# Key indicators by one unsigned comparison, mask rows by DMA, weights in quarters, and where x is transposed, in a fused block-sparse attention and feed-forward kernel

## The chip, the core and the metric

The kernel runs on one NeuronCore of a Trainium2 chip. A core has five engines that run side by side, each with its own instruction queue: TensorE (PE, matrix products, and transposes as products with an identity), VectorE (DVE), ScalarE (ACT, activation functions), GpSimd (POOL) and SyncE (SP, which here only issues transfers). Sixteen DMA engines move data; a transfer is issued from the queue of SP, POOL or ACT and then runs by itself. Matrix products write to PSUM, a small memory of banks that PE, DVE and ACT share; the rest lies in SBUF, 128 partitions wide.

The metric is device time in microseconds (us), the median of several runs.

## What is computed

Attention over four batches of eight heads, 768 positions of 64 numbers each, followed by a gated feed-forward layer. A key block of 32 positions is visible from a query block if it is a neighbour, if either is the first or the last of the 24 blocks, or if it is one of three sampled blocks.

```python
def _attn_ref(q, k, v, sampled_blocks):          # q, k, v: 4 x 8 x 768 x 64
    scores = scale * np.matmul(q, k.transpose(0, 1, 3, 2))
    mask = np.abs(blk_i - blk_j) <= 1
    mask = mask | (blk_i == 0) | (blk_j == 0) | (blk_i == 23) | (blk_j == 23)
    for qb in range(24):
        for kb in sampled_blocks[qb]:
            mask[qb * 32:(qb + 1) * 32, kb * 32:(kb + 1) * 32] = True
    attn = softmax(np.where(mask, scores, -1e9))
    return np.matmul(attn, v)

def _moe_ref(x, w_gate, w_val, w_out, rms_g):    # x: 3072 x 512; w_gate, w_val: 512 x 1536
    xn = x / np.sqrt(np.mean(x * x, axis=-1, keepdims=True) + 1e-06) * rms_g
    g = xn @ w_gate
    return (g * sigmoid(g) * (xn @ w_val)) @ w_out
```

## The kernel before

**Groups.** The queries are worked through in nine groups (L51): three of 256 queries for batch 0 (groups 0, 1, 2), then two of 384 for each other batch. Each group runs its eight heads in order (the loop at L545 to L626). For a head, `scores` (L289) multiplies keys by queries into a PSUM tile `st` and ACT takes the exponential into `ex`. One head later, `pv` (L305) multiplies `ex` by the values `Vp` (whose last column is ones, so that the softmax sum comes out as well), and DVE divides into `stage`.

**The mask is part of the product.** `KT` and `QT` hold 64 rows of keys or queries and 24 further rows. In `KT` these are indicators (row r is 1 where the key lies in block r), in `QT` they are 0 where block r may be seen and -65536 where not. So one product over 88 rows gives masked scores. The positions are interleaved: column s of chunk c stands for position 6 s + c. The rows are built once, in head 0 of the first buffer: `kind` by `mask_keys` (L206, L208) from an integer table `ki_i` that POOL's iota makes (L160), `qmask` by `mask_queries` (L213, L216) from `qnat`, which comes from the small 24 x 24 table `bm` (L184 to L197). Then they are copied to the other seven heads, by DVE (`copy_rows`, L220, L222) or by DMA on SP's queue (L246, L475), and to the second buffer, which batches 1 and 3 use, by two DMAs (L480).

**The head of the kernel.** Batch 0's first two heads of keys and queries come by their own loads and are cast by ACT and turned by PE (`first_cast`, `first_turn`, `first_copy`; `first` in L114 to L119); the other heads of batch 0 come by POOL's queue, which casts on the way (`load_qk`, L72), and are turned by PE in `transpose_qk` (L250, copies at L266) during group 0. Values come by `load_v` (L80) and are cast by DVE in `cast_v` (L103). The weights `wg`, `wv` come in two halves each (`load_gv`, L93), `wo` in one. All loads of one queue keep their order. `keep_busy` (L146) issues products that nobody reads (`unread`), where PE would be idle; `thin` (L557) says in which heads.

**The feed-forward layer as filling.** A group's x is ready when its last head has been divided. `squares` (L319) sums its squares on DVE, `rms_power` (L327) takes the power on POOL, and `rms_scale` (L335 ff.) scales it on DVE into `xs`. Then `xs` has to be turned, so that features lie on partitions, into `xg`. Groups 0, 1 and the last do this on PE (`transpose_x`, L352: eight or twelve transposes in two halves, with the scale `rmsg` applied in DVE's copies at L365); the others scale by `gain` too (L342) and let a DMA on SP's queue transpose (L345). `enter` (L438) then puts the group's feed-forward pieces (`gate`, `val`, `down`; L376, L386, L402) into the list `fill`, and `position()` (L443), called four times a head, takes pieces from it at the rate that empties the list in the given number of positions. So PE alternates between the next group's attention and the last group's feed-forward layer. What is left of the last group runs at the end.

**The order is written by hand** (`manual_schedule`, L58): each engine executes its instructions in program order and waits only for what it needs. An instruction that waits holds up all behind it on its engine.

**Places that the change touches.** In group 0: the prologue (L155 to L247), head 0's turn of the second head (L563 to L574), `side_work` (L461), and the copies in head 2 (L598). In group 1: x of group 0, whose two scalings come at the end of head 0 (L620 to L623) and whose transposes come at the end of head 1 (`tx` is 1 there, L554, L601, L609), with 36 positions. In group 3: x of group 2, by DMA (`by_dma`, L335).

Of the kernel before, what the change touches and what calls it, by code (L numbers as in the profile page):

```python
# [11 lines left out]
I32 = mybir.dt.int32  # L12
AF = mybir.ActivationFunctionType
ALU = mybir.AluOpType
# [3 lines left out]
def kernel(  # L18
# [71 lines left out]
    NWC = 2  # L90
    WC = DFF // NWC

    def load_gv(j):  # L93
        for t, src in ((wg, moe_w_gate), (wv, moe_w_val)):
            nc.gpsimd.dma_start(
                out=t[:, :, j * WC:(j + 1) * WC],
                in_=src.rearrange("(c p) f -> p c f", p=P)[:, :, j * WC:(j + 1) * WC])
# [58 lines left out]
    nc.gpsimd.iota(kq_i[0:NB, :], pattern=[[1, NB]], base=0, channel_multiplier=-1)  # L156
    kc_i = const.tile([32, 1], I32, name="kc_i")
    nc.gpsimd.iota(kc_i[0:NB, :], pattern=[[0, 1]], base=0, channel_multiplier=1)
    ki_i = const.tile([32, S], I32, name="ki_i")
    nc.gpsimd.iota(ki_i[0:NB, :], pattern=[[1, NB], [0, 32]], base=0, channel_multiplier=-1)  # L160
# [6 lines left out]
    load_gv(0)  # L167
# [3 lines left out]
    for i in range(2):  # L171
# [4 lines left out]
    mid = (NB - 1) / 2.0  # L176
    nc.vector.tensor_scalar(out=rg[0:NB, :], in0=kc[0:NB, :], scalar1=-mid, scalar2=None,
                            op0=ALU.add)
    nc.vector.tensor_tensor(out=rg[0:NB, :], in0=rg[0:NB, :], in1=rg[0:NB, :], op=ALU.mult)
    nc.vector.tensor_scalar(out=rg[0:NB, :], in0=rg[0:NB, :], scalar1=(mid - 0.25) ** 2,  # L180
                            scalar2=None, op0=ALU.is_ge)
    kq = const.tile([32, NB], FP32, name="kq")
    nc.vector.tensor_copy(out=kq[0:NB, :], in_=kq_i[0:NB, :])
    bm = const.tile([32, NB], FP32, name="bm")  # L184
    nc.vector.tensor_tensor(out=bm[0:NB, :], in0=kq[0:NB, :], in1=kq[0:NB, :], op=ALU.mult)
    nc.vector.tensor_scalar(out=bm[0:NB, :], in0=bm[0:NB, :], scalar1=1.5, scalar2=rg[0:NB, :],
                            op0=ALU.is_le, op1=ALU.max)
    nc.vector.memset(bm[0:NB, 0:1], 1.0)
    nc.vector.memset(bm[0:NB, NB - 1:NB], 1.0)
    samp = const.tile([32, NB, NRND], FP32, name="samp")  # L190
# [12 lines left out]
    kind = KT[0][D:KR, 0, :]  # L203
    qmask = QT[0][D:KR, 0, :]

    def mask_keys(lo, hi):  # L206

        nc.vector.tensor_scalar(  # L208
            out=kind.rearrange("p (c r) -> p c r", c=NC)[:, lo:hi, :],
            in0=ki_i[0:NB, :].rearrange("p (r c) -> p c r", c=NC)[:, lo:hi, :],  # L210
            scalar1=0.0, scalar2=None, op0=ALU.is_equal)

# [14 lines left out]
    mask_keys(0, HC)  # L227
    unread2 = ps_s.tile([P, 2, 512], FP32, name="unread0", tag="st")
    unread = unread2[:, 0, :]
    for _ in range(4):  # L230
        keep_busy(1, 256, unread)
        for e in range(2):
            nc.tensor.matmul(out=unread2[:, e, 0:256], lhsT=idle[e * D:(e + 1) * D, 0:P],
                             rhs=idle[e * D:(e + 1) * D, 0:256], start=True, stop=True)
# [11 lines left out]
    nc.sync.dma_start(out=KT[0][D:KR, 6:H, :],  # L246
                      in_=kind.unsqueeze(1).to_broadcast([NB, H - 6, S]))  # L247
# [87 lines left out]
    def by_dma(e):  # L335
        return e["grp"] not in (groups[0], groups[1], groups[-1])
# [124 lines left out]
    def side_work(gi, h):  # L461

        if gi == 0:
            if h == 0:
                copy_rows(KT, kind, 2, 4, 0, S)
                copy_rows(QT, qmask, 2, 4, 0, 2 * P)
            if h % 2 == 0:
                cast_v(0, h // 2, nc.vector)
            if h == 1:
                load_gv(1)  # L470
                nc.gpsimd.dma_start(out=wo, in_=moe_w_out.rearrange("(c p) f -> p c f", p=P))
# [6 lines left out]
            if h == 5:  # L478
                for T, m in ((KT, kind), (QT, qmask)):
                    nc.sync.dma_start(out=T[1][D:KR, :, :],  # L480
# [197 lines left out]
```

## Time and profile before

| what | us |
|---|---|
| median of three runs (lowest, highest) | 315.83 (315.8, 316.31) |
| the profiled execution, its own time | 317.69 |
| span of that execution in the profile | 315.9 |
| PE busy (share of the span) | 305.8 (97%) |
| DVE busy | 205.5 (65%) |
| ACT busy | 207.4 (66%) |
| POOL busy | 47.3 (15%) |
| first scores of group 0 on PE | 6.27 |
| transposes of x of group 0 on PE | 28.78 |
| first gate product | 30.26 |
| gate product of group 2 | 83.60 |

The page of a profile gives busy time by engine, the chain of work that ended last (followed back from the last instruction, at each step to what released it), and groups of instructions by line, engine and tile: busy time, mean duration of one in ns, and how long the engine sat idle before them and for whom. The timeline lists instructions in order: start in us, duration in us, engine, line, operation, output and inputs with their shapes, how many are merged, and in brackets the idle time before and what ended it. PEld is the loading of a product's stationary operand, which overlaps other products. SPq is a transfer issued by SP. In the list of stretches each line is: the stretch, its length, and for PE, PEld, DVE, ACT and POOL the busy time (with instructions in brackets), then PE's granted clock, the share of the DMA engines that were busy (above 1 means that packets overlap) and GB/s. Lines beginning with q1 give a hardware DMA queue in a window: packets, MB, busy share of 16 engines. The unread products count as busy too.

### The profile page before, as it was taken

Reading aid. Unit: us, or ns where it says so; the run is one execution under the profiler, and the core shown is the slowest. Engines: PE = TensorE matmul, PEld = TensorE weight load, DVE = VectorE, ACT = ScalarE, POOL = GpSimd, SP = SyncE. Lnnn points to the kernel's source line nnn. Section 1 sums busy time; section 2 is a strip of 40 time slices with the busy share of each in tenths; the row PEclk is TensorE's granted clock in tenths of the full one; section 3 lists DMA queues with packets and bytes.
Section 4 is the critical chain, followed back from the end, with each engine's and each line's share of the span. In section 5 each row is a group of like instructions: output and inputs, shape, how many; then the busy total and the mean of one; then the engine's idle time right before and its main releaser. Section 6 shows DMA issues by size and latency. Waiting matters only on the chain.

```text
span 315.9 us, 7285 instructions
## 1 busy us (share of the span) xinstructions
PE 305.8 (97%) x2869; PEld 200.5 (63%) x2869; DVE 205.5 (65%) x563; ACT 207.4 (66%) x336; POOL 47.3 (15%) x70
## 2 busy tenths in 40 slices
PE   8888999999899999999999999999999999989995
PEld 4566886886588556655666566655666566645653
DVE  7987875678367657682767457683767546683860
ACT  6687776677688676676766766766767666722331
POOL 9705221000220122012020122010000100010000
PEclk9999999999999999999999999999999999999999
DMA  7999999997779487705784288814000230002002
GB/s 143 297 242 212 209 247 188 162 201 131 190 134 164 86 183 152 133 20 130 160 163 100 50 192 125 152 38 118 33 2 0 48 105 2 3 0 100 2 0 101
DMA packets 66766, 37.24 MB, mean 118 GB/s; under 512 B 49532, under 2 KB 62444, under 8 KB 66732
## 3 DMA queue, kind: packets, MB, share of 16 engines
q1 hardware_dynamic: 53000, 19.59, 29.2%
q0 software_dynamic: 13696, 17.17, 28.6%
q8 instruction: 22, 0.36, 0.5%
q14 instruction: 12, 0.10, 0.1%
q10 hardware_dynamic: 36, 0.01, 0.0%
HBM read 28.59 MB, written 6.29 MB: 110 GB/s over the span
## 4 chain that ended last, share of the span: by engine, by line
PE 89%; DVE 7%; DMA 2%; ACT 1%; issue 1%; POOL 0%; DVEq 0%; ACTq 0%
PE gp L379 20%; PE vp L390 19%; PE st L298 19%; PE yp L407 18%; PE op L310 11%; DVE junk L322 2%; DMA xg<-xs 2%; PE unread L151 1%; PE tx L361 1%; DVE stage L315 1%; ACT ex L301 1%; DVE KT L208 0%; DVE u L394 0%; PE tqk L261 0%; DVE KT L266 0%
## 5 line engine op out<-in xcount | busy, mean ns | idle before, releaser
L301 ACT ACTIVATE ex<-st 128x768 bf16<-128x768 f32 x192 | 154.4, 812 | 58.1 <-PE st L298 56.0
L298 PE MATMUL st<-QT,KT 88*128 88x384 bf16 (+1 forms) x432 | 94.6, 309 | 0.8 <-ACT ex L301 0.4
L394 DVE SCALAR_TENSOR_TENSOR u<-th,gp 128x384 bf16<-128x384 bf16 (+1 forms) x108 | 54.8, 508 | 43.1 <-ACT th L383 41.5
L379 PE MATMUL gp<-xg,wg 128*128 128x384 bf16 (+1 forms) x432 | 80.4, 307 | 1.2 <-DMA xg<-xs 1.2
L390 PE MATMUL vp<-xg,wv 128*128 128x384 bf16 (+1 forms) x432 | 80.1, 307 | 0.4 <-DVE u L394 0.4
L407 PE MATMUL yp<-wo,hps 128*128 128x512 bf16 (+1 forms) x300 | 74.0, 370 | 0.7 <-DVE hps L396 0.7
L383 ACT ACTIVATE th<-gp 128x384 bf16<-128x384 f32 (+1 forms) x108 | 48.9, 453 | 28.0 <-PE gp L379 27.8
L396 DVE TENSOR_TENSOR hps<-u,vp 128x384 bf16<-128x384 bf16 (+1 forms) x108 | 55.1, 510 | 11.7 <-PE st L298 0.5
L298 PEld LDWEIGHTS <-KT 88*128 88x128 bf16 x432 | 41.6, 98 | 26.9 <-DVE QT L222 1.3
L379 PEld LDWEIGHTS <-wg 128*128 128x128 bf16 x432 | 40.2, 97 | 21.9 <-DMA xg<-xs 1.3
L390 PEld LDWEIGHTS <-wv 128*128 128x128 bf16 x432 | 40.5, 97 | 20.8 <-issue 0.8
L310 PEld LDWEIGHTS <-ex 128*128 128x128 bf16 x1152 | 46.1, 98 | 11.5 <-DVE stage L315 1.3
L310 PE MATMUL op<-Vp,ex 128*128 128x65 bf16 x1152 | 48.8, 194 | 1.1 <-DVE stage L315 0.6
L407 PEld LDWEIGHTS <-hps 128*128 128x128 bf16 x300 | 27.7, 97 | 23.7 <-DVE hps L396 1.2
L314 DVE RECIPROCAL rz<-op 128x3 f32<-128x3 f32 (+1 forms) x72 | 12.5, 173 | 29.0 <-PE op L310 28.8
L330 POOL TENSOR_TENSOR rstd<-ssq,mhalf 128x3 f32<-128x3 f32 (+1 forms) x9 | 7.3, 814 | 150.0 <-DVE ssq L322 150.0
L315 DVE TENSOR_TENSOR stage<-op,rz 128x192 bf16<-128x192 f32 (+1 forms) x72 | 24.1, 335 | 2.5
L413 ACT ACTIVATE yo<-yp 128x512 f32<-128x512 f32 (+1 forms) x25 | 14.4, 577 | 17.0 <-PE yp L407 17.0
L83 POOL DMA_DIRECT2D vraw<-in_v_dram x16 | 12.0, 748 | 70.9 <-DVE Vp L104 70.7
L322 DVE CUSTOM_DVE_ANT_0 junk<-stage 128x448 bf16<-128x448 bf16 x24 | 14.9, 623 | 0.6
L342 DVE SCALAR_TENSOR_TENSOR xs<-stage,rstd,gain 128x512 bf16<-128x512 bf16 x17 | 11.8, 748 | 4.5 <-POOL rstd L330 4.4
L151 PE MATMUL unread<-idle 128*128 128x512 bf16 (+1 forms) x37 | 12.6, 391 | 1.2 <-DVE idle L144 1.2
(61 smaller groups left out, 98.7 us busy)
## 6 DMA issues: line engine op xcount, KB each, us to landing
vraw<-in_v_dram POOLq DMA_DIRECT2D x16, 384.0 KB, 4.9
out_dram<-yo SPq DMA_DIRECT2D x23, 256.0 KB, 2.3
kbf<-in_k_dram POOLq DMA_DIRECT2D x15, 192.0 KB, 6.2
qbf<-in_q_dram POOLq DMA_DIRECT2D x15, 192.0 KB, 6.5
KT<-turned SPq DMA_DIRECT2D x24, 96.0 KB, 3.6
QT<-turned SPq DMA_DIRECT2D x24, 96.0 KB, 2.4
wg<-in_moe_w_gate_dram POOLq DMA_DIRECT2D x2, 768.0 KB, 16.4
wv<-in_moe_w_val_dram POOLq DMA_DIRECT2D x2, 768.0 KB, 20.2
```

Of the source, the lines that this page charges most:

```text
L151: nc.tensor.matmul(out=t[:, 0:cols], lhsT=idle[:, 0:P], rhs=idle[:, 0:cols], start=True, stop=True)
L298: nc.tensor.matmul(out=at[:, e, 0:tg], lhsT=KT[b % 2][0:KR, h, jt * P:(jt + 1) * P], rhs=QT[b % 2][0:KR, h, c0 * P:c0 * P + tg], start=Tru ...
L301: nc.scalar.activation(out=ex[:, nj * part:nj * (part + 1), :], in_=at[:, 0:nj, 0:tg], func=AF.Exp, scale=SCALE)
L310: nc.tensor.matmul(out=op[:, it, 0:VW], lhsT=ex[:, jt, it * P:(it + 1) * P], rhs=Vp[b % 2][:, h, jt, :], start=(jt == 0), stop=(jt == NC - 1))
L315: nc.vector.tensor_tensor(out=stage[:, 0:n, h * D:(h + 1) * D], in0=op[:, 0:n, 0:D], in1=rz[:, 0:n].unsqueeze(2).to_broadcast([P, n, D]), ...
L322: nc.vector.tensor_tensor_reduce(out=junk[:, 0:hi - lo], in0=part, in1=part, scale=1.0, scalar=(e["ssq"][:, it:it + 1] if lo else DM * 1e- ...
L379: nc.tensor.matmul(out=gp[:, 0:tg], lhsT=wg[:, c, f * P:(f + 1) * P], rhs=xg[:, c, 0:tg], start=(c == 0), stop=(c == KD - 1))
L383: nc.scalar.activation(out=th[:, 0:tg], in_=gp[:, 0:tg], func=AF.Tanh, scale=0.5)
L390: nc.tensor.matmul(out=vp[:, 0:tg], lhsT=wv[:, c, f * P:(f + 1) * P], rhs=xg[:, c, 0:tg], start=(c == 0), stop=(c == KD - 1))
L394: nc.vector.scalar_tensor_tensor(out=u[:, 0:tg], in0=th[:, 0:tg], scalar=1.0, in1=gp[:, 0:tg], op0=ALU.add, op1=ALU.mult)
L396: nc.vector.tensor_tensor(out=hps[:, f, 0:tg], in0=u[:, 0:tg], in1=vp[:, 0:tg], op=ALU.mult)
L407: nc.tensor.matmul(out=yp, lhsT=hps[:, f, tt * P:(tt + 1) * P], rhs=wo[:, f, lo:hi], start=(f == 0), stop=(f == NF - 1))
```

## The change

- **Tables.** Three integer tables of POOL's are made with other bases, and one is added (`kw_i`), so that read as unsigned numbers one comparison says whether a value lies in a range: |a - b| <= 1 becomes (a - b + 1) <= 2 unsigned. In `ki_i` the order of elements becomes that of `kind`, so it is read without a stride.
- **Order in the prologue.** The first half of the indicators is computed ahead of the sampled blocks' part; eight full unread products replace twelve, of which eight used half the rows.
- **Mask rows.** Query rows of the first 256 columns go to heads 2 to 7 by one DMA on SP's queue, issued after `mask_queries(0)`; DVE's copies of them (heads 2 and 3 in head 0, 4 to 7 in head 2) go. The key rows' DMA takes heads 4 to 7 instead of 6 and 7; DVE's copy for 4 and 5 goes. The rows of the second buffer are moved from SP's queue in group 0, head 5, to POOL's queue in group 2, head 1.
- **Turn of the second head.** DVE's row copies for head 1 come ahead of the turn's copies, and one of the four copies is ACT's.
- **`rmsg`** is scaled at the end of group 0 instead of in head 0.
- **Weights.** The first halves of `wg` and `wv` come in two quarters each.
- **x of group 0** is scaled in heads 0 and 1 of group 1 and turned at the start of head 2 (both halves at once), again with 36 positions; head 2 is `thin` too. **x of group 2** is turned by PE.

```diff
-    def load_gv(j):
+    def load_gv(lo, hi):
...
-                out=t[:, :, j * WC:(j + 1) * WC],
+                out=t[:, :, lo * P:hi * P],
...
-    nc.gpsimd.iota(kq_i[0:NB, :], pattern=[[1, NB]], base=0, channel_multiplier=-1)
+    nc.gpsimd.iota(kq_i[0:NB, :], pattern=[[1, NB]], base=1, channel_multiplier=-1)
...
+    nc.gpsimd.iota(kw_i[0:NB, :], pattern=[[0, 1]], base=-1, channel_multiplier=1)
...
-    nc.gpsimd.iota(ki_i[0:NB, :], pattern=[[1, NB], [0, 32]], base=0, channel_multiplier=-1)
+    nc.gpsimd.iota(ki_i[0:NB, :], pattern=[[1, NC], [NC, P]], base=0,
+                   channel_multiplier=-32)
...
-    load_gv(0)
+    load_gv(0, NF // 4)
+    load_gv(NF // 4, NF // 2)
...
-    nc.vector.tensor_scalar(out=rg[0:NB, :], in0=kc[0:NB, :], scalar1=-mid, scalar2=None,
-                            op0=ALU.add)
-    nc.vector.tensor_tensor(out=rg[0:NB, :], in0=rg[0:NB, :], in1=rg[0:NB, :], op=ALU.mult)
-    nc.vector.tensor_scalar(out=rg[0:NB, :], in0=rg[0:NB, :], scalar1=(mid - 0.25) ** 2,
+    nc.vector.tensor_scalar(out=rg[0:NB, :], in0=kw_i[0:NB, :].bitcast(U32), scalar1=NB - 2.5,
                             scalar2=None, op0=ALU.is_ge)
-    nc.vector.tensor_copy(out=kq[0:NB, :], in_=kq_i[0:NB, :])
-    nc.vector.tensor_tensor(out=bm[0:NB, :], in0=kq[0:NB, :], in1=kq[0:NB, :], op=ALU.mult)
-    nc.vector.tensor_scalar(out=bm[0:NB, :], in0=bm[0:NB, :], scalar1=1.5, scalar2=rg[0:NB, :],
-                            op0=ALU.is_le, op1=ALU.max)
+    nc.vector.tensor_scalar(out=bm[0:NB, :], in0=kq_i[0:NB, :].bitcast(U32), scalar1=2.5,
+                            scalar2=None, op0=ALU.is_le)
+    nc.vector.tensor_scalar(out=bm[0:NB, :], in0=bm[0:NB, :], scalar1=rg[0:NB, :],
+                            scalar2=None, op0=ALU.max)
...
+            in0=ki_i[0:NB, :].bitcast(U32).rearrange("p (c r) -> p c r", c=NC)[:, lo:hi, :],
+            scalar1=31.5, scalar2=None, op0=ALU.is_le)
+
+    mask_keys(0, HC)
...
-    mask_keys(0, HC)
-    unread2 = ps_s.tile([P, 2, 512], FP32, name="unread0", tag="st")
...
+    nc.sync.dma_start(out=QT[0][D:KR, 2:H, 0:2 * P],
+                      in_=qmask[:, 0:2 * P].unsqueeze(1).to_broadcast([NB, H - 2, 2 * P]))
+    unread = ps_s.tile([P, 1024], FP32, name="unread0", tag="st")
+    keep_busy(8, 256, unread)
...
-    nc.sync.dma_start(out=KT[0][D:KR, 6:H, :],
-                      in_=kind.unsqueeze(1).to_broadcast([NB, H - 6, S]))
+    nc.sync.dma_start(out=KT[0][D:KR, 4:H, :],
+                      in_=kind.unsqueeze(1).to_broadcast([NB, H - 4, S]))
...
-        return e["grp"] not in (groups[0], groups[1], groups[-1])
+        return e["grp"] not in groups[:FIRST] and e["grp"] != groups[-1]
...
-                copy_rows(QT, qmask, 2, 4, 0, 2 * P)
...
-                load_gv(1)
+                load_gv(NF // 2, NF)
...
-            if h == 5:
-                for T, m in ((KT, kind), (QT, qmask)):
-                    nc.sync.dma_start(out=T[1][D:KR, :, :],
-                                      in_=m.unsqueeze(1).to_broadcast([NB, H, S]))
...
+        if gi == 2 and h == 1:
+            for T, m in ((KT, kind), (QT, qmask)):
+                nc.gpsimd.dma_start(out=T[1][D:KR, :, :],
+                                    in_=m.unsqueeze(1).to_broadcast([NB, H, S]))
...
-        tx = 1 if gi == 1 else TX
...
+                copy_rows(KT, kind, 1, 2, 0, S)
+                copy_rows(QT, qmask, 1, 2, 0, 2 * P)
                 for which in range(2):
                     for w in range(2):
                         first_copy(1, which, second[which], w, 0, 1 if which else HC,
-                                   nc.vector.tensor_copy)
-                copy_rows(KT, kind, 1, 2, 0, S)
-                copy_rows(QT, qmask, 1, 2, 0, 2 * P)
-                nc.vector.tensor_scalar(out=rmsg, in0=rmsg, scalar1=float(DM) ** 0.5,
-                                        scalar2=None, op0=ALU.mult)
+                                   nc.scalar.copy if w > which else nc.vector.tensor_copy)
...
-            if h == tx and ending is not None and tx > 1:
+            if h == TX and ending is not None:
                 transpose_x(ending, 0)
+                if gi == 1:
+                    transpose_x(ending, 1)
+                    enter(ending, NPOS + 4)
+                    ending = None
...
-            if gi == 0 and h == 2:
-                copy_rows(KT, kind, 4, 6, 0, S)
-                copy_rows(QT, qmask, 4, H, 0, 2 * P)
-            if h == tx == 1 and ending is not None:
-                transpose_x(ending, 0)
...
+            if gi == 0 and h == H - 1:
+                nc.vector.tensor_scalar(out=rmsg, in0=rmsg, scalar1=float(DM) ** 0.5,
+                                        scalar2=None, op0=ALU.mult)
```

## The prediction

> **What bounds the kernel.** I read the share of busy time first, then the chain that ended last, then busy time by stretch, then the timeline where that shows TensorE (PE) idle.
>
> ```profile
> PE 89%; DVE 7%; DMA 2%; ACT 1%; issue 1%; POOL 0%; DVEq 0%; ACTq 0%
> ...
> L379 PE MATMUL gp<-xg,wg 128*128 128x384 bf16 (+1 forms) x432 | 80.4, 307 | 1.2 <-DMA xg<-xs 1.2
> ...
> L361 PE MATMUL tx<-ident,xs 128*128 128x128 bf16 x8 | 0.8, 222 | 1.2 <-DVE xs L348 1.2
> ```
>
> PE carries the end. Its waits are small, and two of them are for x: 1.2 us for the DMA that transposes it, 1.2 us for the DVE scaling ahead of PE's own transposes. By stretch:
>
> ```profile
> 28.00:30.00 2.00, 1.03 (x12) 0.86 (x13) 1.86 (x7) 0.25 (x1) 2.00 (x4) 1.00 1.17 216
> 30.00:32.00 2.00, 2.00 (x27) 1.67 (x26) 1.17 (x5) 1.79 (x3) 1.96 (x3) 1.00 1.16 207
> ```
>
> The first number after the length is PE's busy time. From 30.4 us PE is full but for 0.4 us near 46.4, 0.9 us at 82.7 and 0.3 us at 112. Before it, PE also runs dummies, so "busy" proves nothing; there the chain goes through DVE. So two questions: how much earlier does the first gate product end, and what changes later. In the head of the kernel:
>
> ```profile
> 4.86 0.82 DVE L208 TENSOR_SCALAR KT<-ki_i 24x384 bf16<-24x384 int32 x1
> ...
> 6.24 0.82 DVE L208 TENSOR_SCALAR KT<-ki_i 24x384 bf16<-24x384 int32 x1
> ...
> 7.10 1.02 SPq L246 DMA_DIRECT2D KT<-KT  x1
> ...
> 8.11 0.72 DVE L141 COPY KT<-tfirst 64x384 bf16<-64x384 bf16 x2 [1.04 <-PE tfirst L132]
> ...
> 10.07 0.50 PE L298 MATMUL st<-QT,KT 88*128 88x256 bf16 x3 [0.32 <-DVE QT L222]
> ...
> 13.00 0.11 PEld L298 LDWEIGHTS <-KT 88*128 88x128 bf16 x2 [0.47 <-DVE KT L266]
> ...
> 15.02 1.10 DVE L104 CAST Vp<-vraw 128x768 bf16<-128x768 f32 x1
> ...
> 17.62 0.22 PEld L298 LDWEIGHTS <-KT 88*128 88x128 bf16 x3 [0.48 <-DVE QT L222]
> ```
>
> The scores of heads 1, 2 and 4 (10.07, 13.0, 17.6 us) all wait for DVE's copies of mask rows or keys. And at the two places of x:
>
> ```profile
> 28.37 0.77 DVE L348 TENSOR_SCALAR xs<-stage,rstd 128x512 bf16<-128x512 bf16 x2
> 28.78 0.23 PE L361 MATMUL tx<-ident,xs 128*128 128x128 bf16 x1 [0.99 <-DVE xs L348]
> ...
> 29.59 1.12 DVE L365 TENSOR_SCALAR xg<-tx,rmsg 128x256 bf16<-128x256 bf16 x4
> ```
> ```profile
> 79.76 2.58 SPq L345 DMA_TRANSPOSE xg<-xs  x2
> ...
> 83.60 0.61 PE L379 MATMUL gp<-xg,wg 128*128 128x256 bf16 x4 [0.91 <-DMA xg<-xs]
> ```
>
> **The change, part by part.**
>
> *Indicators.* On DVE four small operations go (pieces of the chain: 0.17, 0.19, 0.12, 0.20 = 0.68 us), one maximum of 24x24 comes (nearest row, the fused one at 2.46: 0.23; take 0.20). Saved 0.48. The key comparison reads contiguously instead of every sixth integer: between 0.28 (half of the 768-element qnat row of 0.55) and 0.82 (no gain); I take 0.45, a little over half the strided cost. The first one moves ahead of the sampled blocks and fills what was saved, so the query mask still ends at 4.94 us; then the turn's copies start at 4.97 instead of 5.71, and the second comparison ends at 6.05 instead of 7.06. The first scores hardly profit: seven dummies of 0.21 us from 4.68 hold PE until 6.16 (scores were at 6.27), and ScalarE's second cast ends at 6.39. Gain 0.1. The fewer dummies ahead are a wash: eight at 0.327 us between starts stand for four rounds of 0.65.
>
> *Head 0 to head 1.* The row copies for head 1 (0.35 + 0.35) now fill DVE's 1.04 us idle before the turn. After the turn (about 8.0) DVE has 0.36 + 0.22 + 0.24, to 8.85; ScalarE has one key copy (row 0.47, or 0.36), behind both exponentials, to about 9.1. The dummies ahead of head 1 (0.43) may take the bank which that copy reads: scores at 9.2 to 9.6 instead of 10.07.
>
> *Head 2, by V.* DVE copies rows for heads 2 and 3 (0.55, to 9.4) and then waits for V of the first pair: issued 3.92, landed 6.1 later, 10.0; one more iota ahead of it on POOL's queue (0.1) and more mask packets beside it make 10.3. Cast 0.57, key copies 1.14: 12.0 instead of 12.96.
>
> *Head 2, by masks.* Query rows for heads 2 to 7 now come through SP's queue, issued about 4.95: 24 rows x 6 heads = 144 packets of 512 B, with no row like it. Near bound: the first loads landed 2.5 to 3.7 us after issue, so 8.7. Far bound: the KT transfer above, issued 7.10, 48 packets, moved only here (windows of 1 us from 11 and from 12):
>
> ```profile
> q1 hardware_dynamic: 21, 0.03, 8.5%
> ...
> q1 hardware_dynamic: 39, 0.04, 14.3%
> ```
>
> That is 4.2 us to the first packet and 30 packets a us; for 144 it makes 4.95 + 4.2 + 4.8 = 13.9. It is nearer to the second (same path), but at 5 us POOL's queue has hardly begun, and later mask packets ran at 67 a us: I take 12.4, so head 2's scores at 12.5 (12.1 to 14.0). The Trainium skill, "DMA: Bandwidth & Descriptors", section on arbitration, says that an engine takes turns between its queues packet by packet. By that alone the rows would not stand behind POOL's backlog and would be there by about 9 us; the KT row speaks against it, and I go by the row. The rows of KT for heads 4 to 7 (96 packets behind these) are wanted at 16.5.
>
> *Heads 2 to 4.* The copies of L222 at 16.68 (0.55 + 0.41) are gone, and ScalarE becomes the limit: from scores at 12.5, two exponentials 12.9 to 14.5, PE's values and scores 0.25, exponential 0.81, query copies 0.73, exponential 0.82: head 4's exponential at 17.15 instead of 18.22. DVE is ready for it even if the cast takes 1.10 again (stage of head 1 at 16.1, values of head 2 to 16.5, scores to 16.9). Gain 1.07, in general 13.57 minus the start of head 2's scores. Heads 4 to 7 keep their work, so it lasts.
>
> *The scale of rmsg* moves into the squares at the end of group 0, where DVE runs without a break from 25.16 to 28.3: 0.17 + 0.03 lost.
>
> *x of the first group a head later* moves no DVE work: the scaled x still ends its chain over stage, squares and POOL's power, and the gate product waits for the last of four copies (0.28 each). PE does one scores part (0.33) inside the wait instead of after it, hidden either way. The positions stay 36. Two dummies come in head 2; the first lies in the wait, the second (0.21) behind the gate product is paid.
>
> *x of the third group by PE.* Goes: 0.91 us of stall, two transposes on SP. Comes: 8 transposes x 0.055 = 0.44 on PE, 4 copies of 0.30 on DVE, idle 2.8 us there; the scaling gets cheaper (0.31 to 0.39 for 0.71). Behind the last two transposes PE has 0.33 + 0.22 of other work against about 0.7 until the last copy: 0.16 of stall. Sum -0.31; without the cover of DVE's idle time it would be nought.
>
> *Weights in quarters.* First needed at 31.25 (value half, landed 11.21 + 18.0 = 29.2): 2 us of slack now, 1 us once x comes earlier, and more since each first quarter lands before the second and 0.58 MB of mask traffic leaves that time. Two more issues of 0.8 us on POOL stand ahead of the second half (wanted after 40 us) and end long before the power at 27.6. Cost 0; if the cover went, PE would wait at 30 us.
>
> *Mask rows of the second buffer* go from SP at 14.4 to POOL at about 51: two issues of 0.8, behind them a V load that waits for DVE until 57.6 anyway. Wanted at 70.8; with the slowest landing of a load then (17.6 us) they come at 69.4. Cost 0. The Trainium skill, "SBUF — State Buffer", on the "DVE blocks DMA" trap, speaks against this move: POOL's descriptors and DVE's fast modes lock each other out, where SP's would not. The 1.10 us cast beside POOL's issue at 14.71 fits, the 0.57 us one beside the issue at 11.21 does not; by the rule up to 0.55 us of DVE would be lost at 51 us, where PE has 1.6 us of other work before it needs DVE.
>
> **Sum.** -1.07 + 0.20 + 0.21 - 0.31 = -0.97 us. The profiled execution took 317.69 us around a span of 315.9, the runs' median is 315.83; I take the difference off the median: 314.9.
>
> **Rivals.** (a) *The head's gain is used up*: V or the rows hold head 2 until 13.0, as now. Then 0.57 is gained by head 4, and the sum is -0.47: 315.4, within what a measurement can tell. For it: DMA is above 100% of its 16 engines from 6 us; against it, V landed at 10.0. (b) *The new wait takes over*: rows for heads 2 to 7 come after 13.4 us, from where every us late is a us lost (sum = start of scores minus 13.47). At 14.0 it is +0.5, at 15.0 +1.5: 317.4. For it, the 4.2 us of the KT transfer and its 30 packets a us; against it, that POOL's queue is nearly empty at 5 us. (c) *The transposes only move the wait*: DVE's copies are late in the third group, whose sum is then nought: 315.2 with the head's gain kept, 315.6 if the first group's chain loses 0.4 too. For it, both chains still end in DVE; against, DVE's idle 2.8 us at 80.8.
>
> **From this to numbers.** Forecast (faster, with c's better half) 0.62; (a) and c's worse half 0.20; (b) and anything like it 0.18. 0.2% is 0.63 us, about what this measurement can tell from nothing: faster means below 315.2, slower above 316.46. Low end: scores of head 2 at 12.1 (-0.4), no stall in the third group (-0.16), ScalarE's copy out of head 1's way (-0.4): 313.9. High end: into (b), rows at 14.0: 316.4.
>
> **What would show it.** Head 2's scores near 12.5, and what releases them (KT, QT by DMA, or V's cast); the comparisons near 0.45; head 4's exponential near 17.2; the first gate product ending near 30 instead of 30.9; no DMA wait at 82; TensorE's transposes 16, not 8. I am wrong if scores of head 2 wait for a QT transfer past 13.4, if DVE's query mask ends later than 4.94, or if PE waits at 70.8 for the second buffer's rows.

## The result and the profile after

The changed kernel takes 317.61 us in the median of six runs (317.04 to 318.35); six runs of the kernel before, on the same chip, take 316.12 (315.8 to 316.54). The ratio is 1.0049, 95% interval [1.0034, 1.0065]: slower by 0.5%, outside the range and on the side that had a chance of 0.18. In a second comparison (experiments 1 and 2) the ratio of the same two kernels is 1.0019 [1.0009, 1.0028]. The sign is the same; the 0.3% between the two comparisons stays unexplained. The ratios leave out runs that are over 1.5% longer than the fastest of their kernel, and the text names these runs by their times.

First the page of the profile after (317.04 us, span 315.3): PE's busy share and share of the chain that ended last, then the gate products with their idle time.

```profile
PE 306.1 (97%) x2875; PEld 202.2 (64%) x2875; DVE 202.4 (64%) x560; ACT 207.7 (66%) x337; POOL 50.0 (16%) x75
...
PE 92%; DVE 3%; DMA 2%; ACT 1%; issue 0%; POOL 0%; DVEq 0%; ACTq 0%
...
L375 PE MATMUL gp<-xg,wg 128*128 128x384 bf16 (+1 forms) x432 | 80.7, 307 | 0.7 <-DMA xg<-xs 0.7
```

PE bounds it still. The stalls for the DMA'd x, 0.91 us in the third group and 0.26 in the fourth, have become one of 0.72 in the fourth, at 110 us. What the change set out to do, it does. The timeline of the head:

```profile
5.55 0.35 DVE L194 TENSOR_SCALAR KT<-ki_i 24x384 bf16<-24x384 uint32 x1
...
8.64 0.48 ACT L140 COPY KT<-tfirst 64x384 bf16<-64x384 bf16 x1
...
10.16 0.56 DVE L103 CAST Vp<-vraw 128x768 bf16<-128x768 f32 x1 [0.66 <-DMA vraw<-in_v_dram]
10.21 0.49 PE L294 MATMUL st<-QT,KT 88*128 88x256 bf16 x3
...
12.36 0.49 PE L294 MATMUL st<-QT,KT 88*128 88x256 bf16 x3
...
17.36 1.02 POOL L466 DMA_DIRECT2D wo<-in_moe_w_out_dram  x1 [0.31 <-DMA vraw<-in_v_dram]
...
18.16 0.58 DVE L103 CAST Vp<-vraw 128x768 bf16<-128x768 f32 x1
```

The comparison takes 0.35 us instead of 0.82, head 2's scores start at 12.36 instead of 13.0, and no transfer of mask rows is waited for. Head 1's scores (10.21, 10.07 before) gained nothing. The two last lines matter below: the issue of `wo`, at 14.08 to 14.7 us before, has moved to 17.36. And the two places of x, in the first and the third group:

```profile
27.43 0.23 PE L357 MATMUL tx<-ident,xs 128*128 128x128 bf16 x1
...
28.80 0.88 PE L375 MATMUL gp<-xg,wg 128*128 128x256 bf16 x4
```
```profile
77.18 0.39 PE L357 MATMUL tx<-ident,xs 128*128 128x128 bf16 x4
...
81.22 0.39 PE L357 MATMUL tx<-ident,xs 128*128 128x128 bf16 x4
...
81.65 0.61 DVE L361 TENSOR_SCALAR xg<-tx,rmsg 128x256 bf16<-128x256 bf16 x2 [1.28 <-PE tx L357]
...
81.77 0.80 PE L375 MATMUL gp<-xg,wg 128*128 128x256 bf16 x4
```

The gate product of the third group starts at 81.77 instead of 83.60. Up to the last exponential the two traces alone make the change look like a gain of 1.2 to 1.6 us, of which 0.6 are left in the spans (315.9 and 315.3). But the execution profiled before took 317.69 us, against a median of 315.83. So the first thing to measure was an ordinary execution.

### The profile page after: what moved, and what is told of

Read it like the earlier page. It is cut to its first block, busy times and chain, and to the rows that moved or that the text cites. A ratio compares the mean times of both kernels' runs of the same rounds, so it can differ in the third digit from the quotient of the medians.

```text
span 315.3 us, 7295 instructions
## 1 busy us (share of the span) xinstructions
PE 306.1 (97%) x2875; PEld 202.2 (64%) x2875; DVE 202.4 (64%) x560; ACT 207.7 (66%) x337; POOL 50.0 (16%) x75
## 4 chain that ended last, share of the span: by engine, by line
PE 92%; DVE 3%; DMA 2%; ACT 1%; issue 0%; POOL 0%; DVEq 0%; ACTq 0%
PE gp L375 20%; PE vp L386 19%; PE st L294 19%; PE yp L403 19%; PE op L306 11%; PE unread L150 2%; DVE junk L318 2%; DMA first<-in_k_dram 1%; DMA xg<-xs 1%; PE tx L357 1%; PE tqk L257 1%; DVE stage L311 1%; DVE u L390 0%; PE tfirst L131 0%; DVE hps L392 0%
## 5 line engine op out<-in xcount | busy, mean ns | idle before, releaser
L379 ACT ACTIVATE th<-gp 128x384 bf16<-128x384 f32 (+1 forms) x108 | 48.9, 453 | 28.6 <-PE gp L375 28.4
L392 DVE TENSOR_TENSOR hps<-u,vp 128x384 bf16<-128x384 bf16 (+1 forms) x108 | 55.1, 510 | 12.5 <-PE st L294 0.5
L310 DVE RECIPROCAL rz<-op 128x3 f32<-128x3 f32 (+1 forms) x72 | 12.5, 174 | 28.8 <-PE op L306 28.4
L150 PE MATMUL unread<-idle 128*128 128x512 bf16 (+1 forms) x43 | 14.1, 406 | 1.2 <-DVE idle L143 1.2
L338 DVE SCALAR_TENSOR_TENSOR xs<-stage,rstd,gain 128x512 bf16<-128x512 bf16 x15 | 10.4, 747 | 4.4 <-POOL rstd L326 4.4
```

Source lines behind the costliest of these rows:

```text
L150: nc.tensor.matmul(out=t[:, 0:cols], lhsT=idle[:, 0:P], rhs=idle[:, 0:cols], start=True, stop=True)
L379: nc.scalar.activation(out=th[:, 0:tg], in_=gp[:, 0:tg], func=AF.Tanh, scale=0.5)
L392: nc.vector.tensor_tensor(out=hps[:, f, 0:tg], in0=u[:, 0:tg], in1=vp[:, 0:tg], op=ALU.mult)
```

## Experiments 1 to 4: the same kernels again, and the unread products

Experiment 1 is the kernel before, 2 the changed kernel, 3 the changed kernel with the old products, 4 the kernel before with the new ones:

```diff
-    for _ in range(4):
-        keep_busy(1, 256, unread)
-        for e in range(2):
-            nc.tensor.matmul(out=unread2[:, e, 0:256], lhsT=idle[e * D:(e + 1) * D, 0:P],
-                             rhs=idle[e * D:(e + 1) * D, 0:256], start=True, stop=True)
+    keep_busy(8, 256, unread)
```

> The kernel before, unchanged, to see a profile of it on the same chip. Its profiled execution so far took 317.69 us and its runs 316.12, so it was a slow one: by the clock theory (TensorE's full clock is granted late in some executions, at 7.73 us in that trace) this run is at 315.8 to 316.5 and its trace shows the full clock earlier, or an equal clock and a span near 314.3 for another reason, which would speak against the theory.

> The changed kernel, unchanged. 317.0 to 318.4 us, ratio 1.003 to 1.007. Clock theory: the full clock comes at 9.5 us or later (9.69 in the first trace), since the eight plain unread products run 0.21 us apart, end at 3.1 us and leave TensorE idle for 0.8 us before the first turn. Rival (the time is lost after the first group): the clock's time is no different from the kernel before, and the distance between the two traces changes after 36 us.

> The changed kernel with the unread products of the kernel before (four rounds of one full and a pair on half the rows, until 3.8 us). Clock theory: the full clock comes a window (about 2 us or more) earlier, and the time falls by 1 to 2.5 us, to 315.0 to 316.4, ratio 0.997 to 1.000. Rival: no difference, 317.5.

> The kernel before with the eight plain unread products of the changed one, and nothing else. Clock theory: slower by 1 to 2.5 us, 317.1 to 318.6, ratio 1.003 to 1.008, with the full clock later. Rival: 316.1, no difference.

Against 35 runs of the kernel before (316.52): experiment 1 0.9995 [0.9985, 1.0006], 2 1.0019 [1.0009, 1.0028], 3 1.0022 [1.0009, 1.0035], 4 1.0018 [1.0006, 1.0031] (one of its twelve runs, left out, took 321.01 us). Putting the old products back (3) brings nothing, and putting the new ones into the kernel before (4) costs 0.6 us, of which its trace shows 0.2 in the head and 0.8 at another place (the DMA'd x, below). The clock theory fails on this: the full clock was granted at 6.01, 8.73, 7.43 and 7.95 us in the traces of experiments 1 to 4, so 1.3 us earlier in 3 than in 2, and 3 is no faster. So the products are not the main cause, and what they cost by themselves isn't settled. My "eight at 0.327 us stand for four rounds" is wrong in any case: the eight run in 1.89 us and leave PE idle for 0.74 us at 3.1 us.

The profile of experiment 1 (316.05 us, span 314.3; the twelve runs lie between 315.74 and 316.94) is the yardstick for all that follows. Its timeline at the third group's x, in order of time:

```profile
77.42 2.58 SPq L345 DMA_TRANSPOSE xg<-xs  x2
...
81.50 0.75 POOL L83 DMA_DIRECT2D vraw<-in_v_dram  x1 [6.43 <-DVE Vp L104]
...
81.91 0.60 PE L379 MATMUL gp<-xg,wg 128*128 128x256 bf16 x4
```

No wait: the stall of 0.91 us that I had taken off isn't there when SP issues the transposes at 77.4 instead of 79.8 us. Against this execution, the start of ACT's n-th exponential tells where the changed kernel (experiment 2, span 315.4) wins and loses:

| place | against experiment 1, us | what it is |
|---|---|---|
| group 0, head 4 (8th, from 0) | -0.70 | the head's gain |
| group 0, head 6 (12th) | -0.31 | PE waited for the cast of V beside the issue of `wo` (shown below) |
| group 1, head 4 (24th), and until 75 us | -0.08 | the unread product of head 2, 0.21 us |
| group 3, head 4 (60th), and to the last | +0.57 | third group's x by PE |
| end | +1.15 | 0.56 more behind the last output |

The head's gain differs from one execution to the next: head 4's exponential starts at 17.36 to 18.22 us in the five profiles with the old head and at 16.76 to 17.57 in the twelve with the new one; the means are 0.64 us apart.

## Experiments 5 to 8: one part each

Experiment 5 is the changed kernel with halves, 6 the changed kernel with the third group's x by DMA, 7 the kernel before with it on PE:

```diff
-    load_gv(0, NF // 4)
-    load_gv(NF // 4, NF // 2)
+    load_gv(0, NF // 2)
```
```diff
-        return e["grp"] not in groups[:FIRST] and e["grp"] != groups[-1]
+        return e["grp"] not in (groups[0], groups[1], groups[-1])
```
```diff
-        return e["grp"] not in (groups[0], groups[1], groups[-1])
+        return e["grp"] not in groups[:FIRST] and e["grp"] != groups[-1]
```

Experiment 8 is the kernel before with the change's tables, order in the prologue, rows by DMA in the head, turn of the second head and `rmsg` (the lines of the diff above); unread products, halves and x as before. Its core:

```diff
+    nc.sync.dma_start(out=QT[0][D:KR, 2:H, 0:2 * P],
+                      in_=qmask[:, 0:2 * P].unsqueeze(1).to_broadcast([NB, H - 2, 2 * P]))
...
-    nc.sync.dma_start(out=KT[0][D:KR, 6:H, :],
-                      in_=kind.unsqueeze(1).to_broadcast([NB, H - 6, S]))
+    nc.sync.dma_start(out=KT[0][D:KR, 4:H, :],
+                      in_=kind.unsqueeze(1).to_broadcast([NB, H - 4, S]))
```

> The changed kernel with the first weights in halves again (two issues fewer on POOL's queue); all else as changed. Theory (the quarters push POOL's issue of the output weights from about 14.8 us to 17.4 to 18 us, onto DVE's cast of the values for head 4, and PE loses 0.4 to 0.5 us in heads 4 to 6): that issue ends before 16 us, the cast at about 18 us takes 0.55 us instead of 1.1, the exponentials of heads 5 to 7 come 0.3 to 0.5 us earlier, and the time falls by 0.2 to 0.5 us against the changed kernel (317.1 in the last comparison): 316.6 to 316.9. Rival (the quarters are hidden, as I predicted): no difference within 0.15 us.

> The changed kernel with x of the third group transposed by DMA again. Theory (PE's eight transposes and the wait behind them cost about 0.65 us, while the DMA costs nothing where it is issued by 77.5 us and up to 0.9 us where SP's queue is late): 0.2 to 0.6 us faster than the changed kernel, 316.5 to 316.9, with no wait of PE for xg near 83 us, or one under 0.4 us. Rival (my prediction: the stall for the DMA is always there, 0.91 us, and the transposes save 0.31): 0.3 us slower than the changed kernel, 317.4.

> The kernel before with x of the third group turned by PE and nothing else changed. Theory (price of the transposes 0.65 us against an average stall of the DMA of 0 to 0.5): 0.2 to 0.6 us slower than the kernel before, 316.7 to 317.1; the exponentials keep their distance to the kernel before until 78 us and then fall behind. Rival (my prediction): 0.31 us faster, 316.2.

> The kernel before with the head's part of the change alone: the unsigned comparisons, query rows for heads 2 to 7 and key rows for heads 4 to 7 by DMA on SP's queue, the order of the second turn's copies with one on ScalarE, rmsg later. Weights in halves, paired unread products, x of the first and third group as before. Theory (the head's gain is real and was spent on the other parts): head 4's exponential at about 16.9 us instead of 17.6, no loss at heads 4 to 6 since the output weights are issued early, and 0.5 to 1.0 us faster than the kernel before: 315.5 to 316.0. Rival (the gain is taken up again at the first group's x, whose chain over DVE doesn't come earlier): within 0.2 us of the kernel before.

**Halves (5):** the trace does what the theory said, the time hardly. In the timelines of experiment 2 and then of experiment 5:

```profile
17.86 1.02 POOL L466 DMA_DIRECT2D wo<-in_moe_w_out_dram  x1 [0.57 <-DMA vraw<-in_v_dram]
18.12 1.11 DVE L103 CAST Vp<-vraw 128x768 bf16<-128x768 f32 x1
...
19.82 0.37 PE L306 MATMUL op<-Vp,ex 128*128 128x65 bf16 x6 [0.42 <-DVE stage L311]
```
```profile
15.28 1.03 POOL L465 DMA_DIRECT2D wo<-in_moe_w_out_dram  x1
...
18.15 0.55 DVE L103 CAST Vp<-vraw 128x768 bf16<-128x768 f32 x1
...
19.28 0.56 PE L305 MATMUL op<-Vp,ex 128*128 128x65 bf16 x12
```

Beside POOL's issue the cast takes 1.11 us, without it 0.55, and PE waits 0.42 us. The Trainium skill, "SBUF — State Buffer", section "Who interferes with whom", states that of DVE in a fast mode and GpSimd the one that starts first keeps the pair of ports that they share, and the other waits; here POOL's issue starts first and it is DVE that waits. At head 4 of group 1 experiment 5 is 0.61 us ahead of the yardstick, experiment 2 0.08. Yet the ratio is 1.0017 [1.0007, 1.0028] (without one of eleven runs, 322.33 us) against 1.0019: no difference that the time shows. The collision isn't in every execution. Of the six profiles with quarters, three (2, 6, 15) have the cast start 0.26 to 0.64 us behind POOL's issue, and it takes 1.07 to 1.11 us; in the other three (the profile after, 3, 11) it starts in the last 0.22 us of the issue and takes 0.55 to 0.58.

**The third group's x.** In the kernel before (7) PE turns it in two halves, and the gate product comes at 82.31 instead of 81.91:

```profile
77.72 0.39 PE L361 MATMUL tx<-ident,xs 128*128 128x128 bf16 x4
...
81.76 0.39 PE L361 MATMUL tx<-ident,xs 128*128 128x128 bf16 x4
...
82.31 0.81 PE L379 MATMUL gp<-xg,wg 128*128 128x256 bf16 x4
```

That costs 0.66 us by the exponentials, steady from 85 us to the last; the ratio is 1.0016 [1.0005, 1.0026], 317.08 us (316.85 to 317.8) against 316.71, whose runs reach 324.55. In the changed kernel (6) the theory's "0.2 to 0.6 us faster" was wrong, and the rival's "0.3 slower" far too little: all six runs take 320.27 to 325.88 us. The head alone (8), expected at 315.5 to 316.0, has seven runs of 315.87 to 316.87 and five of 318.99 to 324.31; the ratio without the three longest, 1.0013 [0.9989, 1.0037], says nothing. Its profiled execution is one of the long ones (324.31): timeline, then PE's busy time and clock in stretches.

```profile
80.32 2.58 SPq L345 DMA_TRANSPOSE xg<-xs  x2
...
80.95 0.75 POOL L84 DMA_DIRECT2D vraw<-in_v_dram  x1 [6.43 <-DVE Vp L103]
...
87.30 1.03 PE L379 MATMUL gp<-xg,wg 128*128 128x256 bf16 x4 [5.78 <-DMA xg<-xs]
```
```profile
84.00:86.00 2.00, 0.00 (x0) 0.00 (x0) 0.00 (x0) 0.00 (x0) 0.00 (x0) 1.00 1.45 163
86.00:88.00 2.00, 0.70 (x4) 0.52 (x5) 0.00 (x0) 0.00 (x0) 0.00 (x0) 0.63 1.18 258
88.00:90.00 2.00, 2.00 (x15) 1.35 (x14) 0.56 (x2) 1.20 (x2) 0.00 (x0) 0.50 0.95 224
```

PE stands for 5.78 us, the granted clock falls to half from 86.5 to 93.4 us, and the exponentials lose 8.8 us in all. The Trainium skill, "TensorE: Matmul & The Clock Gate", Part 1, gives half clock after an idle window of about 3.4 us; here it came 5.0 us after PE's last product, and in the other four traces with such a wait (6, 11, 12, 13) 2.5 to 4.6 us after it; the 2.5 us of experiment 12 are less than such a window. Up to there this execution was 0.55 us ahead of the yardstick. So the head's gain is real in the trace, and with it the long wait comes more often. The likely reason: PE comes earlier, but the transposes do not, for they stand on SP's queue behind the turns of batch 1's keys and queries, for whose landings SP waits (4.7 us between 50 and 83 us here, 1.5 in experiment 1). DVE's cast, earlier too, lets POOL's next loads start sooner. Why SP waits longer in some executions isn't shown.

## Experiments 9 to 12: the order on SP's queue

In group 2, one keys or queries pair of batch 1 a head is turned by a DMA transpose into `turned` (L274 before) and, a head later, placed into `KT` or `QT` by two more transfers (L283), all on SP's queue. Experiments 9 (kernel before), 10 (experiment 8) and 11 (experiment 6) issue the last two placings later, 12 is experiment 8 with POOL's loads a head later:

```diff
+        if gi in (FIRST - 1, FIRST) and h == (H - 1 if gi < FIRST else 0):
+            return
         if ready is not None:
             place(*ready)
...
+            if gi == FIRST and h == 1:
+                while turned:
+                    place(*next(iter(turned)))
```
```diff
-        if gi + 1 < FIRST or h not in (2, 4):
+        if gi + 1 < FIRST or h not in (2 + (gi == FIRST), 4 + (gi == FIRST)):
```

> The kernel before with one thing moved on SP's queue: the last two placings of batch 1's keys and queries (first wanted at about 91 us) go behind the two transposes of the third group's x. Theory (those transposes are issued 1.4 to 2.8 us earlier, so they are done before POOL's loads for the next batch start at about 81.5 us): issue by 77 us, no wait of PE for xg at 82 us, 0 to 0.3 us faster than the kernel before in the median (316.3 to 316.7 where the kernel before shows 316.7), and no execution above 318. Rival (the lateness comes from the DMAs' own duration, not from the queue's order): same as before, executions above 320 included.

> The head's part of the change alone (as in the fourth run of the last set) with that order on SP's queue. Theory: the 0.55 us that the head alone had gained at 75 us now lasts to the end, 0.5 to 0.9 us faster than the kernel before (315.8 to 316.2 where it shows 316.7), no execution above 318: a version that beats both. Rival (whatever is gained in the head is lost at the DMA'd x in any order): within 0.2 us of the kernel before, with executions above 320.

> The changed kernel with the third group's x by DMA (324.1 us in the last set) and that order on SP's queue; nothing else differs from that run. Theory: 8 to 9 us come back in one step, 316.2 to 316.8, xg issued near 79 us and landed before the loads do much. Rival (the changed kernel delays SP or the DMA in another way, for instance by the second buffer's mask rows on POOL at 50 us): still above 319.

> The head's part alone in the old order on SP's queue, with DVE's casts and POOL's loads of values, keys and queries a head later in the fourth group (heads 3 and 5 for 2 and 4), so that no load starts beside the transposes of x. Theory (it is the loads that make a late transpose take 7 us instead of 2.5): PE still waits up to 1 us for xg where SP's queue is late, but no execution is above 318.5, median 315.9 to 316.6. Rival (the transposes are slow by themselves, or beside the output's transfers): executions above 320 as often as in the last set (5 of 12).

Experiment 9: 1.0 [0.9984, 1.0016], two of twelve runs at 323.7; no gain, and the theory's "no execution above 318" is wrong (where the long ones lose it, its profile, of a short one, doesn't show). Experiment 10: 316.11 us, 0.9988 [0.9977, 0.9998], one of eleven runs at 321.52. This is the one version whose interval lies below the kernel before, by some 0.4 us, less than hoped; its profiled execution is no shorter than experiment 1's (spans 314.4 and 314.3). Experiment 11: 316.35 us, 0.9995 [0.9982, 1.0007], where experiment 6 took 324.11: the order alone gives nearly 8 us back, though one run of twelve (the profiled one) takes 324.61, since SP's chain itself was late there. Experiment 12 got worse: all five runs take 323.66 to 327.08. Its trace has the wait in two parts, 1.24 us in the third group, where no load is near, and 3.86 in the fourth, where the moved loads have delayed the next turns. That supports the loads as the cause, though the output's transfers, which the rival names too, were not moved, and it shows that moving the loads moves the trouble. All traces in which a DMA turns the third group's x, together (us; "ahead" is from SP's first issue of x's transposes to POOL's next issue of a V load):

| execution | x issued | V load issued | ahead | PE's wait |
|---|---|---|---|---|
| experiments 9, 10 | 76.09, 76.65 | 81.25, 81.82 | 5.2 | 0 |
| experiment 13 | 76.66 | 81.37 | 4.7 | 0 |
| experiment 1 | 77.42 | 81.50 | 4.1 | 0 |
| experiment 14 | 78.55 | 81.00 | 2.5 | 0.83 |
| experiment 4 | 79.21 | 81.70 | 2.5 | 0.79 |
| profile before | 79.76 | 82.12 | 2.4 | 0.91 |
| experiment 12 | 79.63 | 88.04 | 8.4 | 1.24 |
| experiment 8 | 80.32 | 80.95 | 0.6 | 5.78 |
| experiment 11 | 81.00 | 81.24 | 0.2 | 6.18 |
| experiment 6 | 81.51 | 81.28 | -0.2 | 8.49 |

A late issue alone brings a wait of about 1 us; a late issue that meets the loads one of 6 to 8, and the clock on top. The median time from issue to landing of x's transposes is 2.5 us in experiment 1 and 7.0 in experiment 6.

Why does experiment 10 not keep all of the head's gain? Its timeline shows another wait:

```profile
30.98 0.61 PE L390 MATMUL vp<-xg,wv 128*128 128x256 bf16 x4 [0.82 <-DMA wv<-in_moe_w_val_dram]
```

With halves, and the second buffer's mask rows still on SP's queue in group 0, the value weights land at 30.94. Experiment 12 has the same wait (0.70); in experiment 8 they land at 29.96 and the product starts at 30.00. In the kernel before they land at 28.6 to 29.4; with the rows moved to POOL at 26.5 to 28.1 as quarters and at 26.2 to 27.9 as halves (5, 13, 14).

## Experiments 13 to 15: all covers at once, and the end

Experiment 13 is experiment 11 with halves and the paired products; 14 is 13 with each placing two turns behind its turn (the last two still go behind x); 15 is the changed kernel with two small loads on SP:

```diff
+        if gi == FIRST - 1 and len(turned) < 2:
+            ready = None
...
-        if gi in (FIRST - 1, FIRST) and h == (H - 1 if gi < FIRST else 0):
+        if gi == FIRST and h == 0:
```
```diff
+        if gi == 1 and h == 6:
+            spare = const.tile([P, NP], FP32, name="spare")
+            for _ in range(2):
+                nc.sync.dma_start(out=spare, in_=moe_rms_g.rearrange("(h p) -> p h", p=P))
```

> The changed kernel with weights in halves, paired unread products, and x of the third group by DMA in the new order on SP's queue (the second buffer's mask rows stay on POOL at 50 us, which leaves DMA time for the weights). Theory (the head's gain is real and was lost to three things that are put right here): no wait for wv at 30 us, none above 0.3 us for xg at 82, exponentials 0.5 to 0.7 us ahead of a typical execution of the kernel before from 35 us on; median 315.7 to 316.1 where the kernel before shows 316.6, an execution above 320 at most once in ten. Rival (something else takes the gain): within 0.2 us of the kernel before.

> The same with each placing of batch 1's keys and queries issued two turns behind its turn instead of one, so that SP doesn't stand waiting for the turn's landing. Theory (SP's chain from 53 us is made of waits for the turns just issued): xg is issued at 75 to 76.5 us, as soon as DVE has scaled it, instead of 76 to 81; no execution above 318, and the same median as h1 or up to 0.2 us less. Rival (the chain is bound by the landing of the loads or by the output's transfers): xg as late as before, and executions above 320 as often.

> The changed kernel with two small loads (2 KB, into a tile that nobody reads) put on SP's queue at about 42 us, where it has nothing to do. Theory (the end is 0.5 us longer because two DMA instructions left SP's queue, so that another stretch of SP's last instructions comes behind the last landing): 3.2 to 3.4 us from the last scaling of an output block to the end instead of 3.85, and 0.4 to 0.6 us less than the changed kernel (317.1): 316.5 to 316.7. Rival (the end depends on what PE did): 3.8 us, and 317.1.

Experiment 13: 316.28 us, 0.9994 [0.9981, 1.0006]; the rival's "within 0.2 us". The covers hold (no wait at 30 or at 82 us), but the exponentials are only 0.12 us ahead at 35 us instead of 0.5 to 0.7, and the profiled execution, the one of twelve above 320, falls into the same hole one group later:

```profile
108.64 4.58 SPq L345 DMA_TRANSPOSE xg<-xs  x3
109.55 0.76 POOL L84 DMA_DIRECT2D vraw<-in_v_dram  x1 [5.69 <-DVE Vp L103]
...
117.00 1.44 PE L379 MATMUL gp<-xg,wg 128*128 128x384 bf16 x4 [6.88 <-DMA xg<-xs]
```

Experiment 14: 317.2 us; five of twelve runs take 322.46 to 326.04, and without them the ratio is 0.9992 [0.9975, 1.0009]. The longer distance between turn and placing made the long wait no rarer: in its profile, of a short run, x is issued at 78.55, not at 75 to 76.5. So the waits that I had named are not what makes the chain late; what does stays open.

Experiment 15 settles the end. The five profiles before it with the third group's x on PE end 3.80 to 3.86 us after ACT's last write of an output block, the others 3.22 to 3.38. The first line of each pair gives the span, the second that write's start, in experiment 1, experiment 7, and experiment 15 (x on PE, but two other transfers added on SP):

```profile
core 0 of [0], span 314.3 us
...
311.00 0.38 ACT L413 ACTIVATE yo<-yp 128x256 f32<-128x256 f32 x1 [0.93 <-PE yp L407]
```
```profile
core 0 of [0], span 315.5 us
...
311.66 0.38 ACT L413 ACTIVATE yo<-yp 128x256 f32<-128x256 f32 x1 [0.93 <-PE yp L407]
```
```profile
core 0 of [0], span 315.2 us
...
311.87 0.38 ACT L409 ACTIVATE yo<-yp 128x256 f32<-128x256 f32 x1 [0.93 <-PE yp L403]
```

That is 3.28, 3.80 and 3.36 us with the spans unrounded. The ratio of experiment 15 is 1.0002 [0.9991, 1.0013], where the changed kernel has 1.0019; its median is 316.83 us (expected 316.5 to 316.7) with three of twelve runs at 321.26 to 325.33, which the ratio leaves out. The number of transfers on SP decides, not what PE did. SP's last instructions are nine waits in a row, one of them for the last output transfer (2.13 us after that start in both), and a pause of 0.36 to 0.38 us. In experiment 1 the pause comes before that landing and four waits after it; in experiment 7 the pause and six waits (0.065 us each) come after it: 0.38 + 0.13 = 0.51 us. All 17 profiles agree: with 124, 123 and 122 transfers on SP the wait for the last output is the sixth, fifth and fourth of the nine, and the end takes 3.22 to 3.38 us; with 121 and 120 it is the third and the second, and the end takes 3.80 to 3.86. What the pause is, the trace doesn't say.

## Why the prediction was wrong

- **The sum's base: wrong, and the main failure.** The sum was made against the profiled execution, and "I take the difference off the median" carried its whole 0.91 us stall over to the median. Experiment 1's ordinary execution has no such stall; how much of one the median execution has isn't shown. The 1.9 us between the profiled execution and the median had announced it. With the stall left out, my own terms make the third group's x a loss of 0.60 us, not a gain of 0.31, and the sum -0.06; with the head's gain at the measured 0.70 it is +0.31.
- **x of the third group by PE: price right, credit wrong, one term missing.** "0.44 on PE" and "0.16 of stall" make 0.60; experiment 7 measured 0.66. Missing was the end: two transposes fewer on SP cost another 0.5 us (7, 15). Rival (c) had the place, but with a sum of nought.
- **"Weights in quarters... Cost 0": wrong in the trace.** I asked only when the issues end, not what DVE does beside them: the issue of `wo` moved onto head 4's cast, which took 0.39 us of the head in experiment 2 (0.34 to 0.40 in the three profiles that have it, where those without it gain another 0.14 to 0.18). The slack of the value weights was right for the whole change: they landed 2.9 and 3.6 us ahead of their first product (experiment 2 and the profile after). "If the cover went, PE would wait at 30 us" came true in experiments 10 and 12, whose second buffer's rows stay on SP: 0.7 to 0.8 us.
- **The head: right.** Predicted 12.5 us for head 2's scores and 17.15 for head 4's exponential, measured 12.36 and 16.94. The rows by DMA came in time; rival (b) didn't happen. Against experiment 1's execution the gain is 0.70 (experiment 2), not 1.07, for there head 4 started at 17.60 instead of 18.22. Head 1's scores, hoped for at 9.2 to 9.6, stayed at 10.21, and the comparison, taken as 0.45, took 0.35. The scale of `rmsg`, put at 0.20, doesn't show in experiment 2. Of the three signs of being wrong that I had named, two didn't come, and the third, the end of the query mask (4.98 instead of 4.94), is 0.04 us late; none of them points at where the time was lost.
- **x a head later, and the second buffer's rows: right.** The unread product of head 2 was put at 0.21, measured 0.23; nothing waited for the rows at 70 us.
- **The unread products as "a wash": not settled** (nothing in experiment 3, up to 0.6 us in 4).

From there the loss follows, for the traces of experiments 2 and 1: -0.70 + 0.39 + 0.23 + 0.65 + 0.58 (rest and end) = +1.15 us. The median execution before stands 0.5 us above experiment 1's profiled one (316.52 against 316.05), which leaves 0.7; the second comparison's medians differ by 0.6. What the first comparison has beyond that (1.5 us) isn't accounted for.

## What to carry to other kernels

Before a stall is credited to a change, look whether it is in an ordinary execution: if the profiled one is slower than the median, its stalls are the first suspects. A gain ahead of a queue that keeps its own pace need not be passed on; it eats that queue's margin, and where the late transfer then met other loads the price jumped from 1 us to 8. So order a queue by when its results are wanted, and ask of each transfer what will be in flight beside it if it is one microsecond late.

## What was not expected of the hardware

- **Two transfers fewer made the kernel 0.5 us longer** (about 3.85 against 3.3 us at the end, five profiles against twelve), by which of SP's closing waits is the one for the last output and where a pause of SP falls among them.
- **A wait costs more than itself,** because the clock falls to half for 6.8 us, most of which comes behind the wait: waits of 3.86, 5.78 and 6.88 us (experiments 12, 8, 13) delay the exponentials by 6.1, 8.8 and 8.4 us.
- **Some runs of one kernel are 3 to 8 us longer than the rest,** and all five that were traced (6, 8, 11, 12, 13) have the long wait. The kernel before had 5 runs of 318.6 us and above in the 122 of the later comparisons, the head alone 5 in 12. A kernel that turns the third group's x on PE isn't safe from it either: the first comparison and experiments 2, 3 and 7 had none in 40 runs, but experiment 5 had one in 11 and experiment 15 three in 12; no trace shows where these lose the time.
